# The second half's factors of x, made on VectorE from a transposed copy of x instead of by TensorE transposes

## The chip, the cores and the metric

One core of a Trainium2 chip runs the kernel. The metric is the device time of one execution in microseconds (us), lower is better. A time of the kernel is the median of several executions; the profile is a separate execution of the same program, recorded by the hardware profiler.

## What is computed

The input x has 2048 rows of 576 numbers. Each row is normalised (mean subtracted, divided by its standard deviation), and two branches read the result: a spectral filter (a two-dimensional real Fourier transform, a product with a complex weight, the inverse transform) and a gated unit with 4608 inner columns.

```python
def _A_ref(x, w_r, w_i):
    X = jnp.fft.rfft2(x, axes=(-2, -1))
    X = X * (w_r + 1j * w_i)
    return jnp.fft.irfft2(X, s=(S, D), axes=(-2, -1))

def _B_ref(x, w_gate, w_up, w_down):
    g = jnp.einsum("bsd,df->bsf", x, w_gate)
    u = jnp.einsum("bsd,df->bsf", x, w_up)
    h = _sigmoid(g) * u
    return jnp.einsum("bsf,fd->bsd", h, w_down)

xn = _layernorm(x, axis=-1)
return x + _A_ref(xn, A_w_r, A_w_i) + _B_ref(xn, B_w_gate, B_w_up, B_w_down)
```

## The kernel before, in words

**Halves, chunks and factors.** The 2048 rows are worked in two halves (called pairs, p = 0 and 1), each of two chunks of 512 rows. A row's 576 columns are split in two halves of 288. So one pair of x is a 2 by 2 block matrix A11, A12, A21, A22 (chunk, then column half). The gate and up products are done by a seven-product scheme for 2 by 2 blocks, which also needs the sums S1 to S4 of those blocks: S1 = A21 + A22, S2 = S1 - A11, S3 = A11 - A21, S4 = A12 - S2. TensorE needs each factor transposed, with the 288 columns on the partitions, and split into a high and a low part that it multiplies separately. The tile X holds seven such factors; each has five slots of 128 partitions by 512 rows: two for the high part, one for the last 32 columns (stored three times: high, high, low), two for the low part. A21 and S3 share one place, so S3 can be written only after the last product with A21.

**Units.** A unit u stands for 128 inner columns. There are 36 per pair: u = 0 to 35 for pair 0 and 36 to 71 for pair 1. From the third unit of a pair on, `unit` does seven products of seven matmuls each, in the order of PRODS: A11, S1, S2, A12, S3, A22, S4, into PSUM banks pA, pE and pB. The first two units of a pair (u = 36 and 37 here) use `plain`: eight products of A11, A12, A21, A22 alone, so that the sums are not needed yet. After each product ScalarE or VectorE reads the bank: ScalarE copies the up result (v) and takes the sigmoid of the gate (g), VectorE adds and multiplies (y), ScalarE makes the high part hh and VectorE the low part hl.

**Down products.** `down` multiplies the hidden values of two units with w_down: twelve matmuls into a PSUM tile po, then one VectorE addition to acc (L755). The tiles po, the transposes px and a few others share two PSUM buffers, so the third of them waits until VectorE has emptied the first. Eight down products of one j (called po16_0 to po16_7 in the lists below) are spread over two units.

**The second half's factors before.** `second_pair` runs inside unit 35. It loads the 1024 rows of pair 1 (eight DMAs, L344, on SyncE's queue) into tiles xa. For each chunk `blocks` calls `prep` (ScalarE normalises a row tile, L413; ScalarE and VectorE make the three-part remainder, L395 and L400) and `fill`: per factor and 256 rows four f32 transposes of 128x128 and two of the remainder on TensorE (L442, L443) into a PSUM tile px, two ScalarE copies to the high parts (L446, L447) and one VectorE subtraction for the low part (L448). `factors` then makes the sums by 16 VectorE operations on row tiles (L425 to L428) and calls `fill` for S1 to S4. Pair 1 has 16 calls of `fill`, eight for the A blocks and eight for the sums.

**What orders the work.** Each engine takes its instructions in order. Generators (`second_pair`, `factors`, the weights' `get_w`) are stepped between the products of a unit, and a scheduler then places each engine's instructions; the lists below show the outcome. The weights of unit 36 (`w<-wsp`, L283) come over the same SyncE queue as the rows. The rows' mean (mv) and reciprocal deviation (rstd) of pair 1 are made during pair 0 by `later_stats`, one row tile every four units; the last step is in unit 32.

Of the kernel before, what the change touches and what calls it, by code (L numbers as in the profile page):

```python
# [9 lines left out]
F32 = mybir.dt.float32  # L10
# [6 lines left out]
P = 128  # L17
# [8 lines left out]
CW = 512  # L26
# [100 lines left out]
def _layout(x, w_r, w_i, w_gate, w_up, w_down):  # L127

    ks = np.concatenate([np.arange(KT * P), np.tile(np.arange(KT * P, HD), 4)])
    w = np.stack([w_gate[COLS], w_up[COLS]]).reshape(2, 2, HD, NF, P)[:, :, ks]  # L130
    w = w[[1, 1, 0, 0], [0, 1, 1, 0]].reshape(4, KT + 1, P, NF, P).transpose(3, 2, 0, 1, 4)
    v = np.stack([w_r, w_i])[:, :, KOF].reshape(2, N1, N2 // 2, 2, KD).transpose(2, 1, 0, 3, 4)
    v = np.broadcast_to(v[:, None], (N2 // 2, 2, N1, 2, 2, KD))
    lay = {"x": x.reshape(S, D)[ROWS][:, COLS].reshape(NT, P, D), "ri": v.reshape(N2 // 2, P, 4 * KD),
           "w": w.reshape(NF, P, 4 * (KT + 1) * P), "wd": w_down[:, COLS].reshape(NF, P, D)}
    return {k: np.ascontiguousarray(a) for k, a in lay.items()}

# [5 lines left out]


@with_exitstack
def spectral_glu_kernel(ctx: ExitStack, tc: tile.TileContext, x, ri, w_in, w_down, out):
    nc = tc.nc
    con = {k: nc.inline_tensor(v, name=f"c_{k}").ap() for k, v in _constants().items()}

# [28 lines left out]
    acc = {}  # L178


    sc1 = tc.dram_tile([N2 * P, NQ], F32, name="sc1")
    sc2 = tc.dram_tile([N2 * P, NQ], F32, name="sc2")
    spill = tc.dram_tile([TPP * P, D], F32, name="spill")
# [748 lines left out]
    def later_stats(t):  # L932
        xt = R["pool"].tile([P, 5, HD], F32, tag="xa", name=f"xt{t}", bufs=TPC)
        xt = xt.rearrange("p a d -> p (a d)")[:, :D]
        load_x(xt, t)
        for _ in range(4):
            yield
        moments(xt, t, R["pool"])
        if t == NT - 1:
            scales(TPP, TPP, R["pool"], False)  # L940

    def blocks(p, c):
        for mm in range(2):
# [6 lines left out]
    def second_chunk():  # L950

        yield from make_p(1)
        yield from blocks(0, 1)

    def second_pair():

        room("x")
        for m in range(TPC):
            new_xs(1, m)
        for c in range(2):  # L960
            for m in range(TPC):
                load_x(XS[m][:, 2 * c:2 * c + 2].rearrange("p a d -> p (a d)"), TPP + c * TPC + m)
        for _ in range(3):
            yield
        for c in range(2):
            yield from blocks(1, c)

    def factors(p):

# [50 lines left out]
    for p in range(PAIRS):  # L1020

        calls = [(0, 0), (1, 0), (0, 1), (1, 1)] if p == 0 else [(0, 0), (0, 1), (1, 0), (1, 1)]
        for n, (f, c) in enumerate(calls):
            u = p * NF + f
            if p == 0 and n >= 2:
                wd = make_d(f)
            elif p and c == 0:
                wd = get_d(u)
            if p == 0 and n == 0:
                sides.append(second_chunk())  # L1030
            if n == 2 - p:
# [27 lines left out]
        for f in range(G, NF):  # L1059
# [80 lines left out]
```

## Time and profile before

| | |
|---|---|
| time, median of 3 executions | 1438.85 us (1438.41 to 1439.46) |
| the profiled execution's own time | 1438.32 us |
| its span, first to last instruction | 1436.5 us |
| TensorE clock granted, mean | 0.998 of full speed |
| busy: TensorE 99%, VectorE 76%, ScalarE 45% | of the span |

The profile names engines PE (TensorE matmul), PEld (its weight loads), DVE (VectorE), ACT (ScalarE), POOL (GpSimd) and SP (SyncE, which issues the DMAs). A row such as `L448 DVE TENSOR_TENSOR X<-px_S,X 128x512 ... x8 | 5.5, 691 | 9.0` gives the line of the kernel, the engine, what is written from what, the shape, the count, the busy time in us and the mean of one in ns, and the idle time of the engine ahead of them. In the chain of waits, a row is start, length, engine, tile and line, and x7 is a run of seven instructions.

### The profile page before, as it was taken

What the parts mean: (1) busy time and instruction counts of PE and PEld (TensorE: products, weight loads), DVE (VectorE), ACT (ScalarE), POOL (GpSimd) and SP (SyncE); (2) the same over time, 40 slices, a digit from 0 to 9 for tenths busy, and PEclk for the clock granted to TensorE, in tenths of its full rate; (3) what the DMA queues carried; (4) which work ended last, traced back from release to release, by engine and by line L of the source; (5) the groups of instructions that cost most, each with busy time, mean ns of one, the idle gap of its engine ahead of it and who ended that gap; (6) DMA issues with size and microseconds to landing.
All of it is one profiled execution on the core that took longest, in us unless ns stands there. A gap on an engine that the chain in (4) does not pass through costs nothing.

```text
span 1436.5 us, 21196 instructions
## 1 busy us (share of the span) xinstructions
PE 1422.8 (99%) x8073; PEld 1252.0 (87%) x8073; DVE 1087.7 (76%) x1734; ACT 653.5 (45%) x1122; POOL 3.3 (0%) x5
## 2 busy tenths in 40 slices
PE   8999999999999999999999999999999999999998
PEld 5888888888888888889888888888888889898997
DVE  7988888888888787766366687767888877766784
ACT  6644444444444444453345454434555534443431
POOL 0000000000000000000000000000000000000000
PEclk9999999999999999999999999999999999999999
DMA  7588677776777776655676766778888787776642
GB/s 247 195 329 313 256 274 264 265 264 255 262 255 271 262 276 232 230 215 181 213 215 204 210 201 207 206 220 269 273 270 269 245 282 243 226 227 195 202 125 83
DMA packets 128325, 338.79 MB, mean 236 GB/s; under 512 B 11872, under 2 KB 49248, under 8 KB 123360
## 3 DMA queue, kind: packets, MB, share of 16 engines
q1 hardware_dynamic: 127296, 336.13, 69.8%
q8 instruction: 64, 1.05, 0.3%
q10 hardware_dynamic: 928, 1.31, 0.2%
q14 instruction: 37, 0.30, 0.1%
HBM read 201.27 MB, written 136.12 MB: 235 GB/s over the span
## 4 chain that ended last, share of the span: by engine, by line
PE 97%; DVE 1%; ACT 1%; issue 0%; DMA 0%; ACTq 0%
PE pB L644 24%; PE po L751 19%; PE pE L644 16%; PE pA L644 16%; PE ps L842 12%; PE pe L602 2%; PE pd L494 2%; PE pc L546 1%; PE pa L506 1%; PE pb L530 1%; PE py L573 1%; PE pf L478 1%; PE pz L585 1%; PE b L900 0%; PE px_S L442 0%; PE px_A L442 0%
## 5 line engine op out<-in xcount | busy, mean ns | idle before, releaser
L644 PE MATMUL pB<-X,w 128*128 128x512 f32 x1484 | 382.4, 394 | 0.0
L644 PEld LDWEIGHTS pB<-X,w 128*128 128x128 f32 x1484 | 267.5, 188 | 49.5 <-ACT v L708 1.3
L644 PE MATMUL pE<-X,w 128*128 128x512 f32 x1064 | 273.1, 393 | 0.0
L644 PE MATMUL pA<-X,w 128*128 128x512 f32 x1008 | 259.7, 394 | 1.9 <-DVE X L448 1.2
L644 PEld LDWEIGHTS pE<-X,w 128*128 128x128 f32 x1064 | 192.8, 188 | 34.0
L644 PEld LDWEIGHTS pA<-X,w 128*128 128x128 f32 x1008 | 184.2, 189 | 35.8 <-DVE X L448 1.9
L751 PE MATMUL po<-wd,hh 128*128 128x288 f32 x1216 | 210.9, 295 | 0.0
L842 PEld LDWEIGHTS ps<-wf,hs 128*128 128x128 f32 x1260 | 188.6, 188 | 19.3 <-DVE qs L852 1.8
L842 PE MATMUL ps<-wf,hs 128*128 128x288 f32 x1260 | 204.2, 296 | 0.3 <-DVE qs L852 0.3
L751 PEld LDWEIGHTS po<-wd,hh 128*128 128x128 f32 x1216 | 184.4, 188 | 11.2
L755 DVE TENSOR_TENSOR acc<-acc,po 128x576 f32<-128x576 f32 x168 | 126.0, 750 | 76.7 <-PE po L751 75.5
L236 ACT ACTIVATE w<-raw 128x768 fp32r<-128x768 f32 (+1 forms) x106 | 100.8, 952 | 94.2 <-PE pE L644 37.9
L751 PE MATMUL po<-wd,hl 128*128 128x288 f32 x608 | 128.9, 293 | 0.0
L852 DVE TENSOR_TENSOR qs<-qs,ps 128x576 f32<-128x576 f32 x112 | 84.1, 751 | 31.1 <-PE ps L842 30.0
L751 PEld LDWEIGHTS po<-wd,hl 128*128 128x128 f32 x608 | 98.7, 189 | 0.0
L852 DVE TENSOR_TENSOR acc<-acc,ps 128x576 f32<-128x576 f32 x90 | 67.5, 750 | 24.2 <-PE ps L842 23.6
L238 DVE TENSOR_TENSOR w<-raw,w 128x512 fp32r<-128x512 f32 (+1 forms) x106 | 81.9, 773 | 3.2 <-ACT w L236 2.9
L729 DVE TENSOR_TENSOR y<-y,g 128x1024 f32<-128x1024 f32 x67 | 81.9, 1222 | 3.2
L709 DVE TENSOR_TENSOR y<-v,pE 128x512 f32<-128x512 f32 x68 | 46.7, 686 | 49.1 <-ACT v L708 48.2
L778 ACT ACTIVATE hs<-y 128x512 fp32r<-128x512 f32 x105 | 64.9, 629 | 38.9 <-DVE y L729 12.4
L712 ACT ACTIVATE g<-pB 128x512 f32<-128x512 f32 x68 | 40.7, 598 | 91.1 <-PE pB L644 91.1
L708 ACT ACTIVATE v<-pB 128x512 f32<-128x512 f32 x68 | 40.7, 598 | 71.9 <-PE pB L644 71.5
(165 smaller groups left out, 1667.9 us busy)
## 6 DMA issues: line engine op xcount, KB each, us to landing
w<-wsp SPq DMA_DIRECT2D x246, 320.0 KB, 3.5
wsp<-w SPq DMA_DIRECT2D x34, 2240.0 KB, 7.8
raw<-in_w SPq DMA_DIRECT2D x34, 768.0 KB, 9.7
wdsp<-wd SPq DMA_DIRECT2D x36, 576.0 KB, 4.6
wf<-tsp SPq DMA_DIRECT2D x60, 288.0 KB, 3.8
wf<-wdsp SPq DMA_DIRECT2D x45, 288.0 KB, 4.0
std<-in_wd SPq DMA_DIRECT2D x36, 288.0 KB, 5.4
ri<-in_ri SPq DMA_DIRECT2D x16, 578.0 KB, 5.3
```

The costliest lines, as they stand in the source:

```text
L236: placed(nc.scalar.activation(o[:, :, :3, :], src, AF.Copy))
L238: placed(nc.vector.tensor_tensor(o[:, :, 3:, :], src[:, :, :KT, :], f32(o[:, :, :KT, :]), op=OP.subtract))
L644: nc.tensor.matmul(bank, w[:, sw, :], X[:, x, sx, :], start=start and j == 0, stop=stop and j == len(STEPS) - 1, skip_group_check=skip)
L708: nc.scalar.activation(v[:, 1], bank["B"], AF.Copy)
L709: nc.vector.tensor_tensor(y[:, 1], v[:, 1], bank["E"], op=OP.add)
L712: nc.scalar.activation(g[:, 1], bank["B"], AF.Sigmoid)
L729: nc.vector.tensor_tensor(y, y, g, op=OP.mult)
L751: nc.tensor.matmul(pd[:, b, :HD], h[i], w[k][b], start=g == 0 and n == 0, stop=g == G - 1 and n == 2)
L755: nc.vector.tensor_tensor(a, a, pd[:, :, :HD], op=OP.add)
L778: nc.scalar.activation(hs[:, 0], src, AF.Copy)
L842: nc.tensor.matmul(pd[:, i, :HD], h[:, a, m], w[:, b], start=q == 0, stop=q == 2)
L852: nc.vector.tensor_tensor(o, o, pd[:, :, :HD], op=OP.add)
```

## The change

For the second half, x is handed to the kernel a second time, transposed and laid out as the factors need it: `xg` holds for each chunk and column half a block of 128 partitions by 3 x 512 numbers (the last third is the 32 last columns four times). The kernel loads four such blocks. Mean and rstd, which the old way applied per partition, now run along the free dimension; so `later_stats` transposes them once (two small TensorE transposes into a PSUM tile `prow`), a ScalarE copy and a DMA bring them to DRAM as rows (`rowd`), and each is loaded back spread over all 128 partitions (tiles `mr`). VectorE subtracts the mean and multiplies by rstd on the whole block, `put` makes the high parts with ScalarE and the low parts with VectorE, and `second_factors` makes S1 to S4 on whole blocks. `blocks`, `prep`, `sums` and `fill` are no longer called for pair 1. A second new input, also named `xt`, is handed over but not read. `second_pair` is stepped once already ahead of unit 35, so its loads stand earlier. Line numbers of the changed kernel are 4 to 49 higher than those of the kernel before.

```diff
+    xt = x.reshape(NT, P, 2, HD)[..., ks].reshape(NT, P, 2, KT + 1, P).transpose(0, 4, 2, 3, 1)
+    xg = xt[TPP:].reshape(2, TPC, P, 2, KT + 1, P).transpose(0, 3, 2, 4, 1, 5).reshape(2, 2, P, (KT + 1) * CW)
...
+    rowd = tc.dram_tile([2, NT, P], F32, name="rowd")
...
         if t == NT - 1:
             scales(TPP, TPP, R["pool"], False)
+            yield
+            pr = pair("prow")
+            rows = R["pool"].tile([NT, 2, P], F32, tag="xa", name="rows", bufs=TPC)
+            for i, v in enumerate((mv[:, :, 0], rstd)):
+                nc.tensor.transpose(pr[:NT, i, :P], v, idf)
+            nc.scalar.activation(rows, pr[:NT, :, :P], AF.Copy)
+            nc.sync.dma_start(rowd.rearrange("i t p -> t i p"), rows)
...
     def second_pair():
         room("x")
-        for m in range(TPC):
-            new_xs(1, m)
         for c in range(2):
-            for m in range(TPC):
-                load_x(XS[m][:, 2 * c:2 * c + 2].rearrange("p a d -> p (a d)"), TPP + c * TPC + m)
-        for _ in range(3):
+            MR[c] = mr = R["pool"].tile([P, 2, CW], F32, tag="mr", name=f"mr{c}", bufs=2)
+            for i in range(2):
+                nc.sync.dma_start(mr[:, i], rowd[i, TPP + c * TPC:TPP + (c + 1) * TPC].rearrange("t p -> (t p)").partition_broadcast(P))
+            for h in range(2):
+                XG[c, h] = a = R["pool"].tile([P, KT + 1, CW], F32, tag="xg", name=f"xg{c}_{h}", bufs=4)
+                nc.sync.dma_start(a.rearrange("p k s -> p (k s)"), xg[c, h])
+        yield
+        for c in range(2):
+            for h in range(2):
+                yield
+                a = XG[c, h]
+                m, r = (MR[c][:, i].unsqueeze(1).to_broadcast([P, KT + 1, CW]) for i in range(2))
+                tc.keep_in_program_order(nc.vector.tensor_tensor(a, a, m, op=OP.subtract))
+                nc.vector.tensor_tensor(a, a, r, op=OP.mult)
+                if (c, h) == (0, 1):
+                    yield
+                put(f"A{c + 1}{h + 1}", a)
+
+    def put(k, a):
+        o, r = X[:, XA[k]], slice(2 * REM, 3 * REM)
+        nc.scalar.activation(o[:, :KT], a[:, :KT], AF.Copy)
+        nc.scalar.activation(o[:KR, KT], a[:KR, KT], AF.Copy)
+        nc.vector.tensor_tensor(o[:, KT + 1:], a[:, :KT], f32(o[:, :KT]), op=OP.subtract)
+        nc.vector.tensor_tensor(o[r, KT], a[r, KT], f32(o[r, KT]), op=OP.subtract)
+
+    def second_factors():
+        A11, A12, A21, A22 = (XG[c, h] for c in range(2) for h in range(2))
+        nc.vector.tensor_tensor(A22, A21, A22, op=OP.add)
+        put("S1", A22)
             yield
-        for c in range(2):
-            yield from blocks(1, c)
+        nc.vector.tensor_tensor(A21, A11, A21, op=OP.subtract)
+        nc.vector.tensor_tensor(A11, A22, A11, op=OP.subtract)
+        put("S2", A11)
+        yield
+        nc.vector.tensor_tensor(A12, A12, A11, op=OP.subtract)
+        put("S4", A12)
+        yield
+        while not done[1]:
+            yield
+        put("S3", A21)
+        yield
...
-                sides.append(factors(p))
+                sides.append(second_factors() if p else factors(p))
...
             if u == NF - 1:
                 sides.append(second_pair())
+                next(sides[-1])
```

**VectorE in unit 35, from the down product po16_4 on.** Before the change the queue of VectorE reads:

```order
L755 TENSOR_TENSOR acc_162<-acc_162,po16_4_5731 128x576
L425 TENSOR_TENSOR xa1_0_5711<-xa1_0_5711 128x288
L425 TENSOR_TENSOR xa1_1_5712<-xa1_1_5712 128x288
L755 TENSOR_TENSOR acc_162<-acc_162,po16_5_5756 128x576
L425 TENSOR_TENSOR xa1_2_5713<-xa1_2_5713 128x288
L425 TENSOR_TENSOR xa1_3_5714<-xa1_3_5714 128x288
L755 TENSOR_TENSOR acc_162<-acc_162,po16_6_5779 128x576
L448 TENSOR_TENSOR X_66<-px1_A11_0_5802,X_66 128x2x256
L400 TENSOR_TENSOR rma1_2_0_5846<-xa1_2_5713,rma1_2_0_5846 128x2x32
L448 TENSOR_TENSOR X_66<-px1_A12_0_5812,X_66 128x2x256
L400 TENSOR_TENSOR rma1_3_0_5850<-xa1_3_5714,rma1_3_0_5850 128x2x32
L709 TENSOR_TENSOR y35_5674<-v35_5673,pE35_5677 128x512
```

With the change the same stretch reads as follows (L759 is the old L755, L713 the old L709):

```order
L759 TENSOR_TENSOR acc_163<-acc_163,po16_4_5740 128x576
L984 TENSOR_TENSOR xg0_0_5686<-xg0_0_5686,mr0_5683 128x1536
L985 TENSOR_TENSOR xg0_0_5686<-xg0_0_5686,mr0_5683 128x1536
L759 TENSOR_TENSOR acc_163<-acc_163,po16_5_5771 128x576
L984 TENSOR_TENSOR xg0_1_5688<-xg0_1_5688,mr0_5683 128x1536
L995 TENSOR_TENSOR X_66<-xg0_0_5686,X_66 128x1024
L996 TENSOR_TENSOR X_66<-xg0_0_5686,X_66 32x512
L985 TENSOR_TENSOR xg0_1_5688<-xg0_1_5688,mr0_5683 128x1536
L759 TENSOR_TENSOR acc_163<-acc_163,po16_6_5796 128x576
L713 TENSOR_TENSOR y35_5699<-v35_5698,pE35_5702 128x512
L995 TENSOR_TENSOR X_66<-xg0_1_5688,X_66 128x1024
L996 TENSOR_TENSOR X_66<-xg0_1_5688,X_66 32x512
```

The small operations between the additions to acc have gone, and long ones on whole blocks stand there.

**TensorE at the end of unit 35, behind po16_6.** Before the change, transposes stand among the products:

```order
L442 MATMUL px1_A11_0_5802<-idf_61,xa1_0_5711 128x128 x2
L443 MATMUL px1_A11_0_5802<-idr_62,rma1_0_0_5795 96x128
L442 MATMUL px1_A11_0_5802<-idf_61,xa1_1_5712 128x128 x2
L443 MATMUL px1_A11_0_5802<-idr_62,rma1_1_0_5799 96x128
L644 MATMUL pB35_5676<-X_66,w35_5559 128x512 x2
L442 MATMUL px1_A12_0_5812<-idf_61,xa1_0_5711 128x128 x2
L443 MATMUL px1_A12_0_5812<-idr_62,rma1_0_0_5795 96x128
L442 MATMUL px1_A12_0_5812<-idf_61,xa1_1_5712 128x128 x2
L443 MATMUL px1_A12_0_5812<-idr_62,rma1_1_0_5799 96x128
L644 MATMUL pB35_5676<-X_66,w35_5559 128x512 x5
```

With the change, behind po16_7, the last products of unit 35 and the first of unit 36 follow one another:

```order
L648 MATMUL pB35_5701<-X_66,w35_5566 128x512 x7
L648 MATMUL pA36_0_5869<-X_66,w36_5727 128x512 x2
L648 MATMUL pE35_5702<-X_66,w35_5566 128x512 x7
L648 MATMUL pA36_0_5869<-X_66,w36_5727 128x512 x12
L648 MATMUL pE36_0_5870<-X_66,w36_5727 128x512 x7
L755 MATMUL po17_0_5902<-wd34_5651,hh34_5677 128x288 x4
L755 MATMUL po17_0_5902<-wd34_5651,hl34_5678 128x288 x2
L755 MATMUL po17_1_5915<-wd34_5651,hh34_5677 128x288 x4
L755 MATMUL po17_1_5915<-wd34_5651,hl34_5678 128x288 x2
L648 MATMUL pE36_0_5870<-X_66,w36_5727 128x512 x7
L648 MATMUL pA36_1_5979<-X_66,w36_5727 128x512 x2
L755 MATMUL po17_0_5902<-wd35_5729,hh35_5865 128x288 x4
```

No transpose is left, two matmuls of pA36 stand ahead of the last product of unit 35 (pE35), and the down products po17 are cut where their second unit's hidden values (hh35) are not there yet.

**SyncE's queue of DMAs, behind the store of unit 35's weights (wsp35).** Before the change:

```order
L267 DMA wsp35_107<-w35_5559 128x4480
L283 DMA w36_5702<-wsp0_72 128x640
L344 DMA xa1_0_5711<-in_x 128x576
L344 DMA xa1_1_5712<-in_x 128x576
L344 DMA xa1_2_5713<-in_x 128x576
L344 DMA xa1_3_5714<-in_x 128x576
```

With the change:

```order
L271 DMA wsp35_108<-w35_5566 128x4480
L974 DMA mr0_5683<-rowd_69 128x512 x2
L977 DMA xg0_0_5686<-in_xg 128x1536
L977 DMA xg0_1_5688<-in_xg 128x1536
L974 DMA mr1_5690<-rowd_69 128x512 x2
L977 DMA xg1_0_5693<-in_xg 128x1536
L977 DMA xg1_1_5695<-in_xg 128x1536
L287 DMA w36_5727<-wsp0_73 128x640 x4
```

The new loads stand right behind that store, and all four parts of unit 36's weights now stand behind them; before, the first part stood ahead of the rows and waited for TensorE to finish unit 34.

More of the change, by code (lines that the diff above doesn't have):

```diff
@@ L133, in _layout @@
     v = np.broadcast_to(v[:, None], (N2 // 2, 2, N1, 2, 2, KD))
-    lay = {"x": x.reshape(S, D)[ROWS][:, COLS].reshape(NT, P, D), "ri": v.reshape(N2 // 2, P, 4 * KD),
+    x = x.reshape(S, D)[ROWS][:, COLS]
+    xt = x.reshape(NT, P, 2, HD)[..., ks].reshape(NT, P, 2, KT + 1, P).transpose(0, 4, 2, 3, 1)
+    xg = xt[TPP:].reshape(2, TPC, P, 2, KT + 1, P).transpose(0, 3, 2, 4, 1, 5).reshape(2, 2, P, (KT + 1) * CW)
+    lay = {"x": x.reshape(NT, P, D), "xt": xt.reshape(NT, P, 2 * (KT + 1) * P), "xg": xg, "ri": v.reshape(N2 // 2, P, 4 * KD),
            "w": w.reshape(NF, P, 4 * (KT + 1) * P), "wd": w_down[:, COLS].reshape(NF, P, D)}
@@ L145, in spectral_glu_kernel @@
 @with_exitstack
-def spectral_glu_kernel(ctx: ExitStack, tc: tile.TileContext, x, ri, w_in, w_down, out):
+def spectral_glu_kernel(ctx: ExitStack, tc: tile.TileContext, x, xt, xg, ri, w_in, w_down, out):
     nc = tc.nc
@@ L953, in second_chunk @@
         yield from blocks(0, 1)
+    XG, MR = {}, {}
     def second_pair():
         room("x")
-        for m in range(TPC):
-            new_xs(1, m)
         for c in range(2):
-            for m in range(TPC):
-                load_x(XS[m][:, 2 * c:2 * c + 2].rearrange("p a d -> p (a d)"), TPP + c * TPC + m)
-        for _ in range(3):
+            MR[c] = mr = R["pool"].tile([P, 2, CW], F32, tag="mr", name=f"mr{c}", bufs=2)
[34 more added lines that the diff above has]
+        while not done[1]:
             yield
-        for c in range(2):
-            yield from blocks(1, c)
+        put("S3", A21)
+        yield
     def factors(p):
```

## The prediction

> **What bounds the kernel now.** The page's busy times come first, then its shares of the chain that ended last.
>
> ```profile
> PE 1422.8 (99%) x8073; PEld 1252.0 (87%) x8073; DVE 1087.7 (76%) x1734; ACT 653.5 (45%) x1122; POOL 3.3 (0%) x5
> PE 97%; DVE 1%; ACT 1%; issue 0%; DMA 0%; ACTq 0%
> ```
>
> TensorE is busy 99% of the span and is 97% of the chain. Whatever is taken off its queue shortens the run, as long as nothing else becomes late. VectorE averages 76%, so the question is what it does at the place of the change. That place is the turn from the first half of the rows to the second. Its chain by line from 642 to 702 us, and some of its pieces (start, length):
>
> ```profile
> by line: PE pE L644 27.0%; PE po L751 26.5%; PE pB L644 17.1%; PE pA L644 14.6%; PE px_A L442 6.0%; PE px_S L442 5.9%; PE px_A L443 1.7%; PE px_S L443 1.6%
> 637.68 1.61 PE pB L644 x7
> 642.48 1.59 PE po L751 x12
> 644.07 0.22 PE px_A L442 x2
> 644.29 0.06 PE px_A L443
> ...
> 685.38 1.59 PE pE L644 x7
> ...
> 693.05 3.17 PE pE L644 x14
> 696.22 1.59 PE pA L644 x7
> ...
> 698.94 1.67 PE pE L644 x7
> ```
>
> All of it is TensorE. The transposes are 6.0 + 5.9 + 1.7 + 1.6 = 15.2% of 60 us, 9.1 us, or 0.57 for each of the 16 calls of `fill`. VectorE in the stretch that will matter, and ScalarE (busy us after the second and third comma pairs):
>
> ```profile
> 637.00:690.00 53.00, 53.00 (x331) 47.31 (x330) 31.33 (x63) 23.75 (x55) 0.00 (x0) 1.00 0.57 197
> ```
>
> VectorE works 31.3 of these 53 us, ScalarE 23.8. The clock granted is 1.00.
>
> **Removed from TensorE.** 96 transposes, **9.1 us**. A product that stands behind transposes also starts less smoothly: the seven matmuls at 698.94 take 1.67 us, those at 685.38, which follow other products, 1.59. With 14 such places at some 0.06 that is another **0.8 us**. Added are two small transposes behind a down product in unit 32: a transpose costs 0.11 (0.22 for two, above), so **0.2 us**. ScalarE's copy of them must leave before the second next po tile, which comes two products later; TensorE has other work until then.
>
> **VectorE, taken away and added.** The groups between 628 and 705 us, by shape (count, busy us, mean ns):
>
> ```profile
> L755 DVE TENSOR_TENSOR acc<-acc,po 128x576 f32<-128x576 f32 x15 | 11.3, 753 | 12.0 <-PE po L751 11.9
> L448 DVE TENSOR_TENSOR X<-px_S,X 128x512 fp32r<-128x512 f32 x8 | 5.5, 691 | 9.0 <-ACT X L447 8.9
> L448 DVE TENSOR_TENSOR X<-px_A,X 128x512 fp32r<-128x512 f32 x8 | 5.4, 688 | 1.9 <-ACT X L447 1.9
> L671 DVE TENSOR_TENSOR y<-g,pE 128x512 f32<-128x512 f32 x4 | 2.8, 688 | 5.2 <-PE pE L644 5.0
> L400 DVE TENSOR_TENSOR rma<-xa,rma 128x64 fp32r<-128x64 f32 x12 | 2.5, 218 | 2.5 <-ACT rma L395 2.5
> L735 DVE TENSOR_TENSOR hl<-y,hh 128x1024 fp32r<-128x1024 f32 x2 | 2.5, 1226 | 0.5 <-ACT hh L734 0.5
> L425 DVE TENSOR_TENSOR xa<-xa 128x288 f32<-128x288 f32 x4 | 1.8, 456 | 1.2 <-ACT xa L413 1.2
> L400 DVE TENSOR_TENSOR rm<-xa,rm 128x64 fp32r<-128x64 f32 x4 | 0.9, 220 | 0.0
> ```
>
> Away go 10.9 (L448), 3.4 (L400) and 16 sums of 0.45 as in L425, 7.2: together 21.5 us. No row has 1536 numbers per partition. From 512 (0.69) to 1024 (1.23) the cost rises by 0.54, so I take 1.23 + 0.54 = 1.77; three operations of 512 would be 2.07, the upper end, and 1.23 is the lower one. There are 8 for mean and rstd and 4 for the sums: 21.2 us. The low parts are 8 of 1024 numbers (1.23, L735) and 8 of 32x512. The latter I take at 0.69 like 128x512, since the number of partitions does not show in these two neighbours:
>
> ```profile
> 618.33 0.55 DVE L240 TENSOR_TENSOR w<-raw,w 32x384 fp32r<-32x384 f32 x1
> 621.04 0.56 DVE L262 TENSOR_TENSOR raw<-raw 128x384 f32<-128x384 f32 x1
> ```
>
> That is 15.4 us, so 36.6 are added for 21.5: **15 us more** on VectorE, and most of it ahead of 690 us. ScalarE gets lighter: 8 normalisations (L413), the remainders and the half-size copies go, and per factor one copy of 1024 and one of 512 numbers come.
>
> ```profile
> L734 ACT ACTIVATE hh<-y 128x1024 fp32r<-128x1024 f32 x34 | 36.0, 1060 | 10.3 <-DVE y L729 10.3
> L667 ACT ACTIVATE g<-pA 128x512 f32<-128x512 f32 x2 | 1.2, 598 | 5.2 <-PE pA L644 5.1
> ```
>
> I take 1.06 and 0.60.
>
> **Are the blocks there in time?** The new loads stand behind the store of unit 35's weights.
>
> ```profile
> 624.42 0.32 SPq L267 DMA_DIRECT2D wsp<-w  x1
> 630.11 4.74 SPq L344 DMA_DIRECT2D xa<-in_x  x8
> wsp<-w SPq DMA_DIRECT2D x34, 2240.0 KB, 7.8
> raw<-in_w SPq DMA_DIRECT2D x34, 768.0 KB, 9.7
> am<-c_am SPq DMA_DIRECT2D x16, 256.0 KB, 3.1
> 631.00:642.00 11.00, 11.00 (x66) 9.89 (x65) 6.53 (x11) 8.56 (x13) 0.00 (x0) 1.00 0.93 330
> ```
>
> Before, the rows were issued at 630.11 behind a wait; now the loads go at 624.7. At 330 GB/s (the last number of the last row) the 2.3 MB of the store, two 256 KB rows and 0.8 MB of the first block need 10.4 us: the first block lands at about 636, the next at 639, the last at 645 and unit 36's four weight parts by 649. The first is used at 638.4, the weights from 649 on, one part after the other. The price of the wait of the rows' DMA to DRAM (in front of unit 35's raw weights on this queue) is some 3 us there, and those weights are read 20 us later.
>
> **VectorE's queue laid out.** I put the new order down by hand from 634.5, each instruction starting when its engine is free and its inputs are there. Two neighbours that do not depend on each other start 0.08 before the recorded end of the first; dependent ones 0.1 after it:
>
> ```profile
> 612.83 0.75 DVE L755 TENSOR_TENSOR acc<-acc,po 128x576 f32<-128x576 f32 x1
> 613.50 0.75 DVE L297 TENSOR_TENSOR wd<-std,wd 128x576 fp32r<-128x576 f32 x1
> ...
> 629.75 0.69 DVE L728 TENSOR_TENSOR y<-v,pE 128x512 f32<-128x512 f32 x1 [0.85 <-PE pE L644]
> 630.54 1.23 DVE L729 TENSOR_TENSOR y<-y,g 128x1024 f32<-128x1024 f32 x1
> ```
>
> From the addition of po16_4 (637.7, when its matmuls end) to the y of unit 36's second chunk, which the matmuls pE37_1 wait for, stand 45 instructions: 12 additions (9.0), seven of y and hl (5.9), 12 whole-block ones (21.2), 7 pairs of low parts (13.4), 49.5 us, less 25 overlaps of 0.08: 47.5, so 685.2 to 685.4. TensorE's own work between the same points is 693.05 - 637.68 = 55.4 less 12 fills (6.8) and their rough starts (0.5): 48.1, so 685.8 to 686.3. **Both queues are full**, and TensorE is ahead by less than 1 us. In between the waits fall so (needed by TensorE / given): pE35's bank 649.3 / 649.4; A21's low part 658.6 / 658.5; hh35 for po17 659.1 / 659.4; hl35 662.0 / 662.1; po17_6's buffer 677.3 / 677.4. That adds up to **0.5 us** of waiting, and each is so near that 0.1 us more per handover shows at once. For what the hand layout leaves out I take **1.0 us**, with 0 and 3.6 as its ends (3.6 is in the rivals).
>
> One rule of the Trainium skill speaks to these handovers; the rows first:
>
> ```profile
> 622.11 0.68 DVE L238 TENSOR_TENSOR w<-raw,w 128x512 fp32r<-128x512 f32 x1
> 622.81 0.42 DVE L240 TENSOR_TENSOR w<-raw,w 32x256 fp32r<-32x256 f32 x1
> ```
>
> The 32-partition operation starts 0.02 after its neighbour's end instead of 0.08 before it, and I have counted no overlap at those. The Trainium skill (VectorE: DVE Perf Modes, section Two Vector instructions with no wait between them) says that an operation that starts in another group of 32 partitions than the one ahead is held until all earlier ones are done. This trace agrees; without the rule the layout would end some 1 us earlier.
>
> **The sum.** 9.1 + 0.8 - 0.2 - 0.5 - 1.0 = 8.2 us less. The profiled execution took 1438.3, so it would be 1430.1; the median of the runs lies 0.5 above that execution (1438.85), so I forecast **1430.6 us**. With no waits and no allowance the gain is 9.7, 1429.1.
>
> **Rivals.**
> - **VectorE's queue sets the pace.** If every one of 25 free neighbours starts 0.1 after instead of 0.08 before the end, the queue grows by 4.5 us, and 0.9 of it is covered: 3.6 lost in place of the 1.0. If the eight operations with a repeated mean or rstd cost 2.07 instead of 1.77, that is 2.4 more. The time is 1433.2 with the first and 1435.6 with both. For it: the queues are equal within 1 us. Against it: the layout is taken from how neighbours run here.
> - **The loads come late and the run gets slower.** Each `mr` load reads 2 KB rows again for all 128 partitions; no row shows such a load. If the two ahead of the first block took as long as the big store (7.8 each), that block would land at about 650. VectorE has no slack, so each us after 638.4 costs one of TensorE: 11 to 12 us lost, more than the 9.2 that are left to lose, **1441**. It decides from a landing at 647.5 on. Against it: a 256 KB load takes 3.1 us here.
>
> This clock row bears on that rival:
>
> ```profile
> 12.00:24.00 12.00, 9.18 (x38) 6.66 (x37) 9.69 (x28) 6.71 (x15) 0.00 (x0) 0.86 0.61 218
> ```
>
> - The stretch where TensorE was busy only 9.2 of 12 us has the granted clock at 0.86 instead of 1.00. The Trainium skill (TensorE: Matmul & The Clock Gate, Part 1) says that an idle window of about 3.4 us halves the clock until it has been busy that long again. By that rule a single long wait in the late case would add an estimated 1.7 us; no run here shows it at this place yet.
> - **Nothing is won.** TensorE reaches unit 38 earlier and then waits for its weights, which queue behind the stores and loads of acc. Unit 38's first part was issued at 678.4, and TensorE wants it at 689.5 instead of 696.2. A part lands 3.5 to 4.2 us after its issue, so 7 us of cover remain. It would give 1438.
>
> ```profile
> 678.43 0.32 SPq L283 DMA_DIRECT2D w<-wsp  x1
> w<-wsp SPq DMA_DIRECT2D x16, 320.0 KB, 4.2
> ```
>
> **How the numbers follow.** The forecast holds 0.62, VectorE setting the pace 0.25, nothing won 0.07, late loads 0.06. The first two are faster by more than 0.2% (2.9 us, about what a measurement of this kernel can tell from no change): 0.87 faster, 0.07 same, 0.06 slower. The range goes from 1428.8, just under the end without waits, to 1435.2, near the far end of the VectorE rival, and leaves out some 0.15.
>
> **What would show it.** No transposes between 642 and 702; VectorE busy nearly without a gap from 638 to 685; the whole-block operations at 1.77; the start of unit 38's first product near 689.5 (696.2 before). TensorE idle ahead of matmuls that wait for VectorE by more than 2 us in sum means the first rival; ahead of VectorE's first whole-block operation a DMA wait means the second.

## The result, and the profile after

The changed kernel takes **1430.47 us** (median of 4, 1430.12 to 1431.99) where the kernel before takes 1438.78 us in the same session (median of 4, 1438.41 to 1439.46): a ratio of 0.9944, 95% interval 0.9927 to 0.9961. Two later sessions gave 0.9942 (0.993 to 0.9955) and 0.9941 (0.9928 to 0.9953). The forecast was 1430.6 us. The profiled execution took 1430.12 us with a span of 1428.3 us, 8.2 us less than before.

The page's busy times, and its shares of the chain that ended last, by engine:

```profile
PE 1413.8 (99%) x7979; PEld 1242.6 (87%) x7979; DVE 1103.2 (77%) x1714; ACT 642.6 (45%) x1083; POOL 3.3 (0%) x5
PE 95%; DVE 3%; DMA 1%; ACT 1%; issue 0%; SPq 0%; DVEq 0%; ACTq 0%
```

TensorE has 94 instructions and 9.0 us less. 96 transposes went and two came. VectorE has 15.5 us more, as laid out. It now holds 3% of the chain and a DMA 1%; before they held 1% and 0%. The chain of the changed kernel from 628 to 702 us shows where (start, length, engine and tile):

```profile
626.18 13.14 DMA xg<-in_xg
...
639.42 1.77 DVE xg L984
...
649.61 0.61 DVE y L713
...
650.27 1.87 PE pE L648 x7
...
687.12 3.17 PE pE L648 x14
690.29 1.59 PE pA L648 x7
```

The end of the run hangs on the load of the first block, then on VectorE's queue until it has emptied unit 35's bank (L713), and from 650.27 on, where the last product of unit 35 may start, on TensorE alone. No transpose is left. The waits of TensorE and its weight loads in 636 to 700 us (total, times, longest) are few, the longest of them:

```profile
PEld pE L648 <- DVE y L713: 1.2, 1, 1.2
PE pE L648 <- DVE y L713: 0.7, 1, 0.7
PEld po L755 <- DVE hl L739: 0.5, 1, 0.5
PEld pA L648 <- DMA w<-wsp: 0.4, 1, 0.4
```

Only the first place, pE35, stops the products themselves. VectorE in the same stretch:

```profile
637.68 0.76 DVE L759 TENSOR_TENSOR acc<-acc,po 128x576 f32<-128x576 f32 x1 [2.44 <-PE po L755]
639.42 1.76 DVE L984 TENSOR_TENSOR xg<-xg,mr 128x1536 f32<-128x1536 f32 x1 [0.99 <-DMA xg<-in_xg]
...
645.22 1.22 DVE L995 TENSOR_TENSOR X<-xg,X 128x1024 fp32r<-128x1024 f32 x1
646.47 0.68 DVE L996 TENSOR_TENSOR X<-xg,X 32x512 fp32r<-32x512 f32 x1
...
685.37 0.69 DVE L675 TENSOR_TENSOR y<-g,pE 128x512 f32<-128x512 f32 x1
```

It waits once, 0.99 us for the block, and then works without a gap of 0.1 us to the end of the queue at 686.06.

**A measure of the stretch.** The time from the addition of po16_4 (the row at 637.68 above) to the first transpose of `pf` behind this stretch leaves out what differs elsewhere in the run. The first rows of `pf`, before and after:

```profile
735.97 0.38 PE L478 MATMUL pf<-idf,eo 128*128 128x128 f32 x2
```

```profile
727.65 0.38 PE L482 MATMUL pf<-idf,eo 128*128 128x128 f32 x2
```

After the change it is 727.65 - 637.68 = 89.97 us. Before, po16_4 also ended at 637.68, where the product behind it starts, so it was 98.29: 8.3 us more. The experiments by the same measure, from one profiled execution each, with TensorE's idle time between 628 and 740 us and the ratio of the times:

| kernel | stretch, us | TensorE idle, us | ratio to the kernel before (95%) |
|---|---|---|---|
| the kernel before | 98.3 | 0.0 | 1 |
| the change (three profiles) | 89.7 to 90.0 | 0.8 to 1.1 | 0.9944, 0.9942, 0.9941 |
| store behind the loads (two) | 88.9 | 0.0 | 0.9934 (0.992 to 0.9947), 0.9937 (0.9925 to 0.995) |
| loads behind the first weight part | 89.2 | 0.0 | 0.9937 (0.9923 to 0.9951) |
| four extra VectorE operations | 92.6 | 2.5 | 0.996 (0.9946 to 0.9974) |
| the same, store behind the loads | 91.6 | 1.8 | 0.9955 (0.9942 to 0.9969) |
| first block loaded third | 93.7 | 2.6 | 0.9963 (0.995 to 0.9977) |
| order fixed | 96.3 | 4.9 | 0.999 (0.9982 to 0.9999) |
| order fixed, four extra operations | 101.4 | 10.4 | 1.0026 (1.0016 to 1.0037) |
| transposes back, unread | 100.2 | 1.4 | 1.0013 (1.0004 to 1.0022) |
| second chunk on GpSimd | 102.9 | 10.4 | 1.0036 (1.0023 to 1.0048) |

### The profile page after: what moved, and what is told of

It is laid out like the page before. It is cut to its first block, busy times and chain, and to the rows that moved or that the text cites. A ratio compares the mean times of both kernels' runs of the same rounds, so it can differ in the third digit from the quotient of the medians.

```text
span 1428.3 us, 20930 instructions
## 1 busy us (share of the span) xinstructions
PE 1413.8 (99%) x7979; PEld 1242.6 (87%) x7979; DVE 1103.2 (77%) x1714; ACT 642.6 (45%) x1083; POOL 3.3 (0%) x5
## 4 chain that ended last, share of the span: by engine, by line
PE 95%; DVE 3%; DMA 1%; ACT 1%; issue 0%; SPq 0%; DVEq 0%; ACTq 0%
PE pB L648 23%; PE po L755 18%; PE pE L648 16%; PE pA L648 16%; PE ps L846 12%; PE pe L606 2%; PE pd L498 2%; PE pc L550 1%; PE pa L510 1%; PE pb L534 1%; DMA xg<-in_xg 1%; PE py L577 1%; PE pf L482 1%; PE pz L589 1%; PE b L904 0%
## 5 line engine op out<-in xcount | busy, mean ns | idle before, releaser
L755 PE MATMUL po<-wd,hh 128*128 128x288 f32 x1216 | 210.8, 295 | 0.0
L755 PEld LDWEIGHTS po<-wd,hh 128*128 128x128 f32 x1216 | 184.2, 188 | 11.6 <-ACT hh L738 0.2
L759 DVE TENSOR_TENSOR acc<-acc,po 128x576 f32<-128x576 f32 x168 | 125.7, 750 | 71.3 <-PE po L755 71.0
L755 PE MATMUL po<-wd,hl 128*128 128x288 f32 x608 | 128.8, 293 | 0.0
L755 PEld LDWEIGHTS po<-wd,hl 128*128 128x128 f32 x608 | 98.7, 189 | 0.5 <-DVE hl L739 0.5
L713 DVE TENSOR_TENSOR y<-v,pE 128x512 f32<-128x512 f32 x68 | 46.8, 688 | 49.0 <-ACT v L712 48.2
```

Of the source, the lines that this page charges most:

```text
L713: nc.vector.tensor_tensor(y[:, 1], v[:, 1], bank["E"], op=OP.add)
L755: nc.tensor.matmul(pd[:, b, :HD], h[i], w[k][b], start=g == 0 and n == 0, stop=g == G - 1 and n == 2)
L759: nc.vector.tensor_tensor(a, a, pd[:, :, :HD], op=OP.add)
```

## The experiments

The theory at the start was that of the prediction: the gain is the transposes' time on TensorE, and VectorE's queue, now as full as TensorE's, gives back a little. The rivals: the gain is from something else in the change (earlier loads, fewer buffers), or VectorE has slack.

**The transposes back, unread.** For each factor `put` first calls `idle_fills`, which does on constants what `fill` put on TensorE, into tiles that nobody reads.

```diff
+    def idle_fills(k, n):
+        for q in range(n):
+            pt = pair(f"pi_{k}_{q}")
+            for j in range(2):
+                for i in range(KT):
+                    nc.tensor.transpose(pt[:, 0, (2 * i + j) * P:(2 * i + j + 1) * P], idf, idf)
+                nc.tensor.transpose(pt[:KR, 1, j * P:(j + 1) * P].bitcast(F32R), idr[:, :KR], idr)
+
     def put(k, a):
 
+        idle_fills(k, 2)
```

> The 96 transposes put back on TensorE, of the identity into PSUM tiles that nobody reads; everything else as changed. Theory (the gain is TensorE time, 9.1 us of transposes and 0.8 of rough starts of the products behind them): 8 to 9.9 us over the changed kernel, since up to 1.3 us of waits for VectorE are covered by them: 1438.5 to 1440.4. Rival (the gain came from ScalarE and VectorE no longer reading transposes out of the two shared PSUM buffers): 4 us or less.

Measured: 1441.24 us (1439.81 to 1443.05), ratio 1.0013 (1.0004 to 1.0022). Against the change's 0.9942 that is 0.0071, 10.2 us, a little over the 8 to 9.9 expected and far from the rival's 4; the stretch is 10.2 to 10.5 us longer, 0.3 to 0.6 of it more idle time than in the change. So the gain is the transposes' time on TensorE. With the transposes back the kernel is 0.13% slower than the kernel before, and the interval excludes 1: what the change brings besides them, the 1.4 us of waits in this kernel among it, costs a little.

**VectorE longer by four operations.** Their result goes to a tile that is not read.

```diff
                 nc.vector.tensor_tensor(a, a, r, op=OP.mult)
+                zz = R["pool"].tile([P, KT + 1, CW], F32, tag="zz", name=f"zz{c}_{h}", bufs=1)
+                nc.vector.tensor_tensor(zz, a, m, op=OP.add)
```

> Four more whole-block VectorE operations, one behind each multiplication by rstd, into a scratch tile that nobody reads. Theory (VectorE's queue from the first block to the start of unit 37's last product is as full as TensorE's): each costs 1.76 us less an overlap of 0.08, 6.7 in all, and at most 1.5 of it is covered: 5.2 to 6.7 us over the changed kernel, 1435.7 to 1437.2. Rival (TensorE alone sets the end, VectorE has room as its busy share of 77% says): 0 to 0.5 us, under 1431.

Measured: 1433.55 us (1432.68 to 1434.89). By the ratios it costs 0.0018, 2.6 us; by the stretch 2.5 to 2.8. Both theory (5 and more) and rival (nothing) miss. The chain of that kernel's profile at the end of VectorE's queue:

```profile
692.19 0.70 DVE y L675
692.93 5.06 PE pE L648 x21
```

VectorE works without a gap from 639.63 and the product pE37_1 waits for it. It starts at 692.93 where the change has 687.12, 5.8 us later, or 5.5 counted from the addition of po16_4. Yet the stretch grew by less than half of that: TensorE's instructions stand in another order here, with unit 38's first product and parts of unit 37 moved ahead of that place. The new theory: VectorE's queue has no slack, but the scheduler, which knows the longer queue, moves products that need nothing of it into the gap. To test it, the order must be held.

**The order held, without and with the four operations.** In units 35 to 38 TensorE's instructions are kept in the order of the code. TensorE's order is then the same in both kernels.

```diff
+    pin = [False]
+    def pinned(ins):
+        if pin[0]:
+            tc.keep_in_program_order(ins)
...
-            nc.tensor.matmul(bank, w[:, sw, :], X[:, x, sx, :], ...
+            pinned(nc.tensor.matmul(bank, w[:, sw, :], X[:, x, sx, :], ...
...
-                    nc.tensor.matmul(pd[:, b, :HD], h[i], w[k][b], ...
+                    pinned(nc.tensor.matmul(pd[:, b, :HD], h[i], w[k][b], ...
...
+            if u == NF - 1:
+                pin[0] = True
             unit(u, beside)
+            if u == NF + G:
+                pin[0] = False
```

> The changed kernel as it is, on the chip of the next three runs, so that these have a base of their own. Every theory expects a ratio of 0.994 to the kernel before, 1430 to 1431.5 us.

> From unit 35 to unit 38 TensorE's products and down products stand in the order in which the code writes them: the product pE35 ahead of all of unit 36, the down products po17 whole behind hh35, no part of unit 38 ahead of unit 37's last product. Nothing else differs. Theory: VectorE's queue is as full as TensorE's, and the interleaved order of the change covers some of the handovers; without it 1 to 4 us more than the change. Rival: that order does nothing, within 0.5 us of the change.

> The fixed order with the four extra whole-block operations on VectorE (their result is not read). TensorE's order is the same instruction by instruction as in the run with the fixed order alone, so the scheduler cannot answer. Theory: the 2.3 to 2.6 us that the four operations cost earlier, in place of 7.0, were small because the scheduler moved unit 38's first product ahead of unit 37's last one; here they cost 5.5 to 7.0 us more than the fixed order alone. Rival: VectorE has some 4.5 us of slack of its own somewhere in the stretch; then they cost 2 to 3 us here too.

Measured: the change 1430.63 us (1429.16 to 1431.76), the fixed order 1437.49 (1436.15 to 1438.43), the fixed order with the extra operations 1442.65 (1441.41 to 1444.51). The extra operations cost 1442.65 - 1437.49 = 5.2 us (5.1 by the stretch), just under the theory's range and far from the rival's 2 to 3; the intervals of the two ratios leave 3.2 to 7.1. What these 5.2 us are made of stands below, behind the fixed order by itself.

The fixed order by itself costs 6.9 us, more than the 1 to 4 expected: it gives back nearly all that the change won. In its profile TensorE stops at pE35 and at the first down products that need hh35 and hl35:

```profile
651.58 1.88 PE L654 MATMUL pE<-X,w 128*128 128x512 f32 x7 [0.93 <-DVE y L719]
...
658.59 0.43 PE L761 MATMUL po<-wd,hl 128*128 128x288 f32 x2
661.19 1.13 PE L761 MATMUL po<-wd,hh 128*128 128x288 f32 x4 [2.17 <-ACT hh L744]
664.14 0.85 PE L761 MATMUL po<-wd,hl 128*128 128x288 f32 x2 [1.83 <-DVE hl L745]
```

In the change these down products are cut in two and stand behind pE36 and parts of pA36 of the second chunk, and no such wait of the products is left. The idle time explains 4.9 - 0.8 = 4.1 us. Two such matmuls take 0.43 at 658.59, ahead of these waits, and 0.85 at 664.14, which is the clock. Its windows (the number behind the five busy times is the granted clock):

```profile
661.15:662.40 1.25, 1.13 (x4) 0.78 (x4) 1.22 (x2) 0.00 (x0) 0.00 (x0) 0.62 0.00 0
664.10:667.60 3.50, 3.46 (x14) 3.46 (x15) 2.32 (x2) 1.58 (x2) 0.00 (x0) 0.50 0.09 36
667.60:669.60 2.00, 2.00 (x10) 1.65 (x9) 1.69 (x2) 0.00 (x0) 0.00 (x0) 0.83 0.26 98
```

At these clocks 1.13 x 0.38 + 3.46 x 0.50 + 2.00 x 0.17 = 2.5 us of work is lost. With the idle time that is 6.6 us; the stretch is 6.3 us longer and the time 6.9. The kernel before was not run with its order fixed, so how much of its time hangs on its own order is not shown.

With the four operations, in the same order, the same three waits are longer:

```profile
651.36 1.88 PE L654 MATMUL pE<-X,w 128*128 128x512 f32 x7 [2.83 <-DVE y L719]
...
662.64 0.79 PE L761 MATMUL po<-wd,hh 128*128 128x288 f32 x4 [3.84 <-ACT hh L744]
667.18 0.85 PE L761 MATMUL po<-wd,hl 128*128 128x288 f32 x2 [3.75 <-DVE hl L745]
```

Each has grown by 1.7 to 1.9 us, about one operation, since ahead of each of the three stands one more of the extra operations. The last of these handovers is hl35. VectorE makes it here, with the order fixed alone and then with the extra operations:

```profile
662.87 1.22 DVE L745 TENSOR_TENSOR hl<-y,hh 128x1024 fp32r<-128x1024 f32 x1
```

```profile
665.91 1.22 DVE L745 TENSOR_TENSOR hl<-y,hh 128x1024 fp32r<-128x1024 f32 x1
...
669.38 1.75 DVE L993 TENSOR_TENSOR zz<-xg,mr 128x1536 f32<-128x1536 f32 x1
```

Counted from the addition of po16_4, hl35 starts at 23.4 and at 28.5 us, 5.2 us later: three operations of 1.75 less an overlap of 0.08 each, and 0.2 us by which the first block started later. The fourth stands behind hl35, and behind hl35 no product waits in either kernel. So VectorE's time is TensorE's, one for one, up to the last handover that TensorE waits for; the fourth operation comes after it and cost nothing that shows.

**The store behind the loads.** The store of unit 35's weights, which stands ahead of the new loads, is issued behind them. TensorE's order stays as in the change.

```diff
-        nc.sync.dma_start(wsp[f], f32(w).rearrange("p a k m -> p (a k m)"))
+        if f < NF - 1:
+            nc.sync.dma_start(wsp[f], f32(w).rearrange("p a k m -> p (a k m)"))
...
                 nc.sync.dma_start(a.rearrange("p k s -> p (k s)"), xg[c, h])
+        nc.sync.dma_start(wsp[NF - 1], f32(WS[NF - 1]).rearrange("p a k m -> p (a k m)"))
```

> The store of unit 35's weights is issued behind the new loads instead of ahead of them. Theory (VectorE starts the first block 1.0 us late because the block lands behind the 2.2 MB of the store, and VectorE has no slack): the DMA wait goes, the first block starts right behind the addition of po16_4, and the waits of TensorE for VectorE shrink by 0.7 to 1.3 us: 1429.2 to 1429.8. Rival (the landing is covered): within 0.2 us of the changed kernel.

> The changed kernel as it is, as the base of the next three runs on the same chip: ratio 0.994 to the kernel before.

> The store of unit 35's weights behind the new loads, measured beside the change on one chip; TensorE's order is the same in both, instruction by instruction. Theory: the 1.0 us by which VectorE starts late and the waits behind it go, 1.0 to 1.5 us less than the change, ratio about 0.9932. Rival: the earlier time came from the chip, within 0.4 us of the change.

Measured: 1429.25 us (1429.04 to 1430.86) in one session; in another 1430.25 (1428.81 to 1431.03) beside the change's 1430.51 (1429.43 to 1431.63). The times alone don't settle it: the ratios, 0.9934 and 0.9937, lie within the change's intervals, and the 0.3 us between the two medians of one session are what the rival expected. The profiles do for the mechanism: the spans are 1427.2 and 1427.0 us where three profiles of the change have 1428.1 to 1428.3 (other executions of the change reach 1427.4, so this alone proves little), the stretch is 1 us shorter, and the chain of the second of them between 628 and 700 us is TensorE alone, with no wait for VectorE or a DMA:

```profile
by line: PE po L756 35.7%; PE pE L649 26.6%; PE pB L649 20.0%; PE pA L649 17.8%; issue 0.0%
```

Of the 112 us from 628 to 740, TensorE is busy for 111.24 in the first profile of the change and for 111.97 here.

So the late first block costs the change about 1 us, and this kernel is the fastest by its profiles, though by its times not provably.

**Both: the store behind the loads and the four operations.**

> The store of unit 35's weights behind the new loads, and the four extra whole-block operations. VectorE starts when po16_4 is added and not 1.0 us later. Theory: VectorE's end sets the pace with these four operations, so the earlier start comes out of the time whole or nearly so: 1.0 to 1.5 us less than the four operations gave without it (ratio to the kernel before 0.9950 to 0.9953 where that was 0.996). Rival: the scheduler's order hides the start; the same as without, 0.996.

Measured: 1431.9 us (1431.36 to 1433.26), ratio 0.9955 (0.9942 to 0.9969); the four operations alone gave 0.996, so the times don't separate the two. In the profiles VectorE starts 0.67 us after po16_4's addition begins instead of 1.60, 0.93 us earlier, and the stretch is 0.93 us shorter. By the profiles the earlier start comes out of the time whole, as the theory says, though the 0.93 us are just under its 1.0 to 1.5; the times don't show it. Against the store behind the loads alone the four operations cost 2.7 us, as they did against the change: over half of their 7 us is covered where the scheduler is free.

**Later loads, in two ways.** First the block that is used first is loaded as the third of the four:

```diff
-            for h in range(2):
-                XG[c, h] = a = ...
-                nc.sync.dma_start(a.rearrange("p k s -> p (k s)"), xg[c, h])
+            for h in range(2):
+                XG[c, h] = a = ...
+        for c, h in ((1, 1), (1, 0), (0, 0), (0, 1)):
+            nc.sync.dma_start(XG[c, h].rearrange("p k s -> p (k s)"), xg[c, h])
```

> The block of A11 is loaded as the third of the four, behind the second pair of rows and two other blocks: 2.1 MB at 330 GB/s, 6.4 us later, at about 645.8. Theory (no slack on VectorE): 5 to 7 us over the changed kernel, 1435.5 to 1437.5, with VectorE waiting for the DMA ahead of its first whole-block operation. Rival (VectorE catches up): 2 us or less.

Then the early step of `second_pair` is left out, so that the loads stand behind the first part of unit 36's weights:

```diff
                 sides.append(second_pair())
-                next(sides[-1])
```

> The early step of the loads is undone: they stand behind the first part of unit 36's weights, which waits for TensorE to leave unit 34, and are issued 5 to 6 us later. Theory: the first block lands at 643 to 645 in place of 639.4; the landing of 645.6 in the run with that block third cost about 2.7 us, so 1.5 to 3 us more than the change. Rival: the scheduler plans for the later loads (it does place pieces of unit 36 and 38 differently) and covers them, under 0.7 us.

Measured: the first 1434.12 us (1434.04 to 1434.24), 3.0 us over the change by the ratios and 3.7 by the stretch, below the 5 to 7 expected. The second 1430.55 (1429.16 to 1431.42) beside the change's 1430.51: nothing, as the rival expected, and the theory's 1.5 to 3 us fall. In both the block starts later after po16_4's addition than the change's 1.74 us: 7.64 and 3.87. VectorE in the two profiles:

```profile
645.57 1.76 DVE L985 TENSOR_TENSOR xg<-xg,mr 128x1536 f32<-128x1536 f32 x1 [3.69 <-DMA w<-wsp]
```

```profile
643.40 1.75 DVE L984 TENSOR_TENSOR xg<-xg,mr 128x1536 f32<-128x1536 f32 x1
```

In the first kernel the profile puts the end of VectorE's wait down to a load of weights; by the landings in the trace it was the block itself, at 645.55, and the weights followed from 648.2 on. In the second kernel VectorE does not wait for the block, since the scheduler has put the addition of po16_5 ahead of it, and 13 matmuls of unit 36 stand ahead of pE35 where the change has two; TensorE is busy all of the 112 us. So the early step by itself wins nothing that these times could show; by the stretch the change, which has it, is even 0.6 to 0.9 us longer. In the first kernel the wait is too long to be covered, and half of its price is the clock again. TensorE and its clock there:

```profile
650.80 0.50 PE L648 MATMUL pA<-X,w 128*128 128x512 f32 x1 [1.72 <-ACT X L994]
```

```profile
648.00:652.50 4.50, 2.63 (x13) 1.77 (x11) 4.47 (x4) 2.06 (x3) 0.00 (x0) 1.00 0.84 326
652.50:655.40 2.90, 2.88 (x7) 2.30 (x8) 2.87 (x3) 0.40 (x1) 0.00 (x0) 0.51 0.04 17
655.40:658.70 3.30, 3.30 (x15) 2.66 (x14) 3.24 (x5) 1.18 (x2) 0.00 (x0) 0.91 0.02 5
```

2.88 x 0.49 + 3.30 x 0.09 = 1.7 us are lost to the clock, and 2.6 - 0.8 = 1.8 us more idle time make 3.5 of the 3.7.

**The second chunk on GpSimd.** Its four operations with mean and rstd leave VectorE.

```diff
-                tc.keep_in_program_order(nc.vector.tensor_tensor(a, a, m, op=OP.subtract))
-                nc.vector.tensor_tensor(a, a, r, op=OP.mult)
+                eng = nc.gpsimd if c else nc.vector
+                tc.keep_in_program_order(eng.tensor_tensor(a, a, m, op=OP.subtract))
+                eng.tensor_tensor(a, a, r, op=OP.mult)
```

> The four operations with mean and rstd of the second chunk are made by GpSimd; VectorE has 7.0 us less. No row of this case shows such an operation on GpSimd. Theory: the change waits for VectorE because its first block lands late, ahead of the second chunk, so at most 0.5 us is gained; if one takes over 4 us there, A21 comes late and it costs 2 us or more. Rival: VectorE's whole queue sets the pace, and 1 us or more is gained.

Measured: 1444.62 us (1442.36 to 1445.22), ratio 1.0036 (1.0023 to 1.0048): 14 us over the change. The cause is not the one expected, that A21 would come late. GpSimd, and VectorE at the same time:

```profile
647.04 3.81 POOL L985 TENSOR_TENSOR xg<-xg,mr 128x1536 f32<-128x1536 f32 x1 [643.22 <-DMA xg<-in_xg]
650.92 3.74 POOL L986 TENSOR_TENSOR xg<-xg,mr 128x1536 f32<-128x1536 f32 x1
654.63 4.96 POOL L985 TENSOR_TENSOR xg<-xg,mr 128x1536 f32<-128x1536 f32 x1
659.67 4.35 POOL L986 TENSOR_TENSOR xg<-xg,mr 128x1536 f32<-128x1536 f32 x1
```

```profile
647.52 3.87 DVE L997 TENSOR_TENSOR X<-xg,X 32x512 fp32r<-32x512 f32 x1
651.42 4.86 DVE L986 TENSOR_TENSOR xg<-xg,mr 128x1536 f32<-128x1536 f32 x1
656.20 0.74 DVE L759 TENSOR_TENSOR acc<-acc,po 128x576 f32<-128x576 f32 x1
...
657.46 3.21 DVE L996 TENSOR_TENSOR X<-xg,X 128x1024 fp32r<-128x1024 f32 x1
660.71 3.86 DVE L997 TENSOR_TENSOR X<-xg,X 32x512 fp32r<-32x512 f32 x1
```

Operations of 0.68, 1.76 and 1.22 us take 3.87, 4.86 and 3.21 while GpSimd works; each ends about when its own duration has passed since the GpSimd operation that was running ended (650.85 + 0.54, 654.66 + 1.62, 659.59 + 1.08). The addition to acc, which reads po from PSUM, keeps its 0.74. VectorE loses 3.2 + 3.1 + 2.0 + 3.2 = 11.5 us for the 7 it was spared, pE35's bank is emptied 6 us late (18.0 us behind po16_4's addition instead of 11.9), so that 7.1 of TensorE's 10.4 us of idle time stand ahead of pE35, and the clock is at 0.50 from 657.5 to 660.7. GpSimd's operations hold waits for VectorE too: less the time until the VectorE operation that was running ended (0.45, 0.47, 1.65 and 1.00, the first behind an L996 that ended at 647.49), they come to about 3.3 us each, an estimate from these rows. The Trainium skill (SBUF — State Buffer, section SBUF: two separate sides) says that VectorE operations with two SBUF inputs and GpSimd operations take turns on a port pair that one holds for its whole instruction. This trace agrees, with the durations above.

## Why the prediction was right, point by point

- **The transposes, 9.1 + 0.8 - 0.2 = 9.7 us.** Right to half a us. The two added transposes lie ahead of the stretch, so 9.9 belong to it; without any wait it is 88.9 us instead of 98.29, 9.4 less. Put back unread, the transposes cost 10.2 us, 0.3 to 0.6 of it waits.
- **The waits, 0.5 us in five places, and the allowance of 1.0.** The total came out by luck. As printed, four of the five places are waits (A21's low part was there in time), and they add up to 0.6 instead of 0.5. In the runs pE35, which was to wait 0.1 us, waits 0.7 and its seven matmuls then take 1.87 instead of 1.59, 1.0 together. The other places cost next to nothing. So 1.0 us is lost where 1.5 was allowed, and 9.4 - 1.0 = 8.4 (measured 8.3 by the stretch) equals 9.9 - 1.5: the two misses of half a us cancel. The cause of the loss, the late block, was not among the waits laid out. The store behind the loads, which takes this one wait away, shows that it hangs on the landing.
- **The landing of the first block at 636.** Wrong: 639.4, so VectorE started 1.0 us late instead of in time. The estimate took 330 GB/s and let the transfers pass one after the other; the sizes that it names, 3.6 MB, need 10.9 us at that rate and not 10.4, which moves it by 0.5. The window from the store's issue to that landing (the last number is GB/s), and the transfers issued between 620 and 660 us (KB each, median us to landing):

```profile
624.40:639.40 15.00, 15.00 (x90) 13.52 (x89) 7.38 (x9) 2.35 (x4) 0.00 (x0) 1.00 0.91 309
632.20:637.40 5.20, 5.20 (x34) 4.79 (x34) 2.18 (x3) 1.21 (x2) 0.00 (x0) 1.00 0.98 264
```

```profile
wsp<-w SPq DMA_DIRECT2D x1, 2240.0 KB, 7.8
mr<-rowd SPq DMA_DIRECT2D x4, 256.0 KB, 12.8
```

  309 GB/s over 15.0 us are 4.6 MB, where the store and the loads up to the first block hold 3.6: the mean rate was nearly as taken, but 1 MB more than those was moved. Most of the delay stands at the two `mr` loads. The store, issued at 624.38, lands 7.8 us later, at 632.2. The two loads land at 635.1 and 637.4, 5.2 us where the estimate has 1.6 for their 0.5 MB, and the block 1.9 us behind them. With the store behind them nothing large is ahead of the `mr` loads, and still the first takes 4.3 us to land; the DMA engines were a quarter busy meanwhile (the last two numbers are their busy share and GB/s):

```profile
624.50:628.80 4.30, 4.30 (x27) 3.87 (x26) 1.90 (x3) 0.60 (x1) 0.00 (x0) 1.00 0.25 95
```

  So such a load takes longer than its bytes ask for even with little beside it; why, and how much the transfers beside it add in the change, no run separates.
- **Durations on VectorE: 1.77, 1.23 and 0.69.** Right: 1.76, 1.22 and 0.68. A factor repeated along the free dimension costs nothing extra: 1.75 to 1.76 with it (L984) and for two full blocks (L1001). The 32x512 operation at 646.47 starts 0.03 behind its neighbour's end, as it was counted.
- **Both queues full.** Right as a layout: VectorE ends at 686.06 (685.2 to 685.4, and 1.0 late at the start), pE37_1 starts at 687.12, unit 38 at 690.29 (689.5). Wrong in "VectorE has no slack, so each us costs one of TensorE". With TensorE's order held it is so up to hl35 and not behind it, 5.2 of 7 us; where the scheduler is free it is 2.6 of 7. By that share the VectorE rival (3.6 us lost in place of 1.0) was priced too high.
- **Late loads.** The direction was right, the price too high: the first block 5.9 us later cost 3.7 us, and 2.1 us later with another order nothing. The 1.7 us put on the clock for a long wait is also what was measured with that block third, but there the pause was 1.7 us, and in another run one of 2.83 us cost nothing on the clock (last section), so the equal size is luck; in the change itself the clock stayed at 1.00 behind pauses of 0.7 to 1.0 us.
- **Nothing won.** Fell: no product stops for its weights; one weight load waits 0.4 us for a DMA, beside the products.
- **What was not seen.** The gain rests on the order in which the scheduler cut the po17 down products. It was read into the layout as given. With the order held the change loses 6.9 of its 8.3 us; 4.0 us of the idle time, and the slow clock behind it, stand at these down products.

## What to carry to other kernels

Work taken from the engine that bounds a kernel shows up whole only if what replaces it keeps every handover; here that was the order of the instructions on TensorE, and without it nearly all of the gain was lost. A delay on the other engine counts only if it stands ahead of a handover that is waited for. When an experiment adds a delay, compare the orders of the two programs first: a scheduler that knows of the delay answers it, and the price is then that of the new order. Price a wait with the clock in it: here 1.8 us of TensorE's idle time cost another 1.7 in slower matmuls, and 4.1 another 2.5; but the length of one pause did not foretell it.

## What the runs showed of the hardware

- **The clock can halve after a pause of about 2 us, and does not always.** With the first block loaded third, a pause of 1.72 us, 1.5 us of work and 0.17 more of pause were followed by 2.9 us at 0.51. With the order fixed, a pause of 2.17 us was followed by a clock of 0.62 and, after a second of 1.83, 3.5 us at 0.50. With the second chunk on GpSimd, a pause of 2.10 us was followed by 0.6 us at 1.00 and 3.5 us at 0.51. But with the order fixed and the four operations, the pause of 2.83 us ahead of pE35 and the 7.4 us of work behind it were at 1.00:

```profile
648.50:651.40 2.90, 0.07 (x2) 0.04 (x1) 2.90 (x4) 1.25 (x2) 0.00 (x0) 1.00 0.78 313
651.40:658.80 7.40, 7.39 (x34) 6.04 (x34) 7.34 (x7) 0.93 (x2) 0.00 (x0) 1.00 0.55 160
```

  Behind the next pause, of 3.84 us, it fell to 0.50 within 1 us. Pauses of 0.7 to 1.0 us at pE35 left it at 1.00. The clock was back at 1.00 some 3 to 4 us after work had resumed (3.1 with GpSimd, 3.5 with the block third, 4.1 with the order fixed). The Trainium skill (TensorE: Matmul & The Clock Gate, Part 1) names an idle window of about 3.4 us; the halving agrees, but the pauses of 1.7 to 2.2 us ahead of it here were shorter than that. What decides it, these runs don't show.
- **GpSimd and VectorE take turns** on operations with two SBUF inputs, as shown above; an elementwise operation of 128x1536 takes 3.7 to 5.0 us on GpSimd, waits for VectorE included, and 1.76 on VectorE alone.
